# A fused cosine attention and two-layer MLP on one core: one pair's normalisation moved behind another quad's scalings, two transposes moved to later groups, weight loads asked for ahead of squares

## The chip, the cores and the metric

The kernel runs on one core of a Trainium2 chip. The metric is the device time of one execution in microseconds (us), lower is better; where several executions were timed, their median is given. The core's engines are TensorE (PE in the profile: matmuls, and PEld for its weight loads), VectorE (DVE), ScalarE (ACT), GpSimd (POOL) and SyncE (SP), which only issues transfers (DMAs). Each engine works through its own list of instructions in order; semaphores make it wait for others.

## The reference

```python
batch, n_heads, seq, head_dim = (8, 12, 448, 64)          # q, k, v
n_tokens, d_model, d_ff = (3584, 768, 2048)               # w_in, w_out
...
q_n = q / (np.linalg.norm(q, axis=-1, keepdims=True) + 1e-06)
k_n = k / (np.linalg.norm(k, axis=-1, keepdims=True) + 1e-06)
scores = np.matmul(q_n, k_n.transpose(0, 1, 3, 2)) / tau
attn = softmax of scores over the keys
attn_out = np.matmul(attn, v)
...
x = attn_out as (batch * seq, heads * head_dim)
h = x @ w_in
g = np.maximum(0.01 * h, h)
out = g @ w_out
```

All inputs are float32, tau is 0.1. Scores of normalised vectors are bounded, so the kernel takes the exponential without subtracting the maximum.

## The kernel before

**Units of work.** Two heads of one batch are a *pair* (48 pairs, `NSLOT`; six per batch), two pairs are a *quad* of four heads (`j`, three per batch). The 448 positions of a head are three blocks of 128 and a rest of 64. Pairs are counted from 0 through the whole kernel: pairs 0 to 5 are batch 0, pair 6 (the seventh) is the first of batch 1. Quad 2 is the last of batch 0.

**Preparing a pair `s`.** Its queries and keys are loaded in float32 into `raw_sb` (six places, used in turn). GpSimd squares them (`squares`, L173 to L184, two operations, one for queries, one for keys and each with part of the rest); VectorE sums each row (`sums`, L186, two reductions); ScalarE takes the root as exp(0.5 ln x) (`roots`, L197). `normalise` (L213 to L228) then runs on VectorE: an addition (L217), a reciprocal (L218) and two multiplications that write the normalised bf16 tile `qn` (L222, 128x512 and 128x384; called the pair's *scalings* here). `transposes` (L248) turns `qn` over: for pairs below 10 by seven small TensorE products (L236) into one bank of PSUM and a copy by VectorE (L260) into `qkT`; from pair 10 on (`DMA_FROM`) by a DMA that SyncE issues. `norm` (L700 to L717) strings these together and lets GpSimd go on: `hold` (L511) is a tiny GpSimd copy that reads a value of `qn[s]`, so all that stands behind it in GpSimd's list waits for that pair's scalings; behind it come squares of a later pair and, for pairs 7 and 8, a quarter of `w_out`.

**Attention.** `key_tiles` (L267) makes the scores of key blocks, keys on the partitions (L279), and ScalarE takes their exponential (L291). The rest blocks of two pairs share a tile (`ki` of 3), which so needs `qkT` of both: the tile called (7, 3) reads pairs 6 and 7, the tile (9, 3) reads pairs 8 and 9. `attend` (L660) sums the exponentials by products with ones and multiplies them with `v` (L319); ScalarE forms the reciprocals `rb` (L338, L339) and VectorE scales the result into `xT` (`scale`, L355 to L362, instruction at L360): the attention output with features on the partitions. Quad 2 fills the last two of the six feature blocks.

**The MLP.** `first` (L374) multiplies one block `m` of 128 of the 2048 inner features: six products (L383), one for each feature block, then ScalarE's leaky ReLU into `hT` (L390). `firsts` (L719) goes through all 16 blocks, called *groups* below; a table `between` says what is emitted ahead of which group. The first four groups of batch 0 (`SOON`) have their first four products done earlier, and need only the last two, those that read quad 2's part of `xT`. `groups` (L441) does the second layer (L458) and `visit` (L729) mixes it with the key tiles of the next batch: first the tiles (7, 3) and (9, 3), then groups of output rows with a key tile every few products.

**Order.** Nothing is left to a scheduler (`manual_schedule`): the order on every engine is the order of emission. PSUM has eight banks, and `banks` (L75) gives out those whose last use was longest ago. GpSimd also issues DMAs: `w_in`, the queries and keys of pairs 10 and 11 (L584 to L586), `w_out` in four quarters named by their first block 0, 4, 8 and 12 (`load_w_out`, L109; the reader is L458), and `v`. SyncE issues the other loads and the stores.

**Around the change.** At the end of batch 0 the list is: `sums(6)`, `sums(7)`, `roots(6)`, `normalise(6)` (L655 to L658); `attend` of quad 2 (L751), with its scalings at the end; a `hold` on `xT`, `w_out` quarter 0, a `hold` on `qn[6]`, `squares(9)`, quarter 4 (L752 to L756); `norm(7)` without its transposes, with `squares(10)` and quarter 8; `sums(8)`; and then the 16 groups of batch 0 with the table at L760 to L769, in which `transposes(6)` to `transposes(9)`, `norm(8)` to `norm(10)` and their sums are spread. Squares 10 and 11 can only begin when their pairs have been loaded.

Of the kernel before, what the change touches and what calls it, by code (L numbers as in the profile page):

```python
# [16 lines left out]
def kernel(  # L17
# [57 lines left out]
    def banks(count, keep=None, which=None):  # L75
        lo, hi = (0, 8) if not deals["apart"] else (0, 4) if count == 2 else (4, 8)
        x = which if which is not None else min(
            (i for i in range(lo, hi, count) if not set(range(i, i + count)) & set(sum(kept.values(), []))),
            key=lambda i: max(age[i : i + count]),
        )  # L80
        deals["n"] += 1
        age[x : x + count] = [deals["n"]] * count
        if keep:
            kept[keep] = list(range(x, x + count))
        return ps[:, x] if count == 1 else ps[:, x : x + count]

    def given_back(keep):
        deals["n"] += 1
        for i in kept.pop(keep):
            age[i] = deals["n"]  # L90
# [18 lines left out]
    def load_w_out(parts):  # L109
        for m in parts:  # L110
            gp.dma_start(out=w_out_sb[:, m : m + MT // 4], in_=w_out_r[:, m : m + MT // 4])

    def main(x, b, h0, nh):
        return x[b, h0 : h0 + nh, 0:MAIN].rearrange("h (p t) d -> p h t d", t=3)
# [40 lines left out]
    def load_v(j):  # L155
        if j >= B * NQ:
            return
        b, jj = divmod(j, NQ)
        vb[j] = vbp.tile([128, 4, 3, D], BF16, name="v_b")
        gp.dma_start(out=vb[j], in_=main(v, b, 4 * jj, 4))  # L160
# [25 lines left out]
    def sums(s, parts=(0, 1)):  # L186
        if s >= NSLOT:
            return
        if s not in ss:
            ss[s] = smp.tile([128, 14], F32, name="ss")  # L190
        for i in parts:
            o = ss[s][:, 0:8] if i == 0 else ss[s][:, 8:14]
            nc.vector.tensor_reduce(  # L193
                o.rearrange("p (h t) -> p h t", h=2), sqs[s][i], axis=AX.X, op=ALU.add
            )

    def roots(s):  # L197
        if s >= NSLOT:
            return
        nc.scalar.activation(ss[s], ss[s], func=AF.Ln, bias=tiny)  # L200
        nc.scalar.activation(ss[s], ss[s], func=AF.Exp, scale=0.5)  # L201
# [11 lines left out]
    def normalise(s):  # L213
        if s >= NSLOT:
            return
        r = smp.tile([128, 14], F32, name="r")
        nc.vector.tensor_scalar_add(ss[s], ss[s], 1e-6)  # L217
        nc.vector.reciprocal(r, ss[s])  # L218
        qn[s] = qnp.tile([128, 7, 2, D], BF16, name="qn")
        for x, lo, hi, r0 in ((raw[s][0], 0, 4, 0), (raw[s][1], 4, 7, 8)):  # L220
            nt = hi - lo
            scalings[s] = nc.vector.tensor_tensor(  # L222
                qn[s][:, lo:hi],
                x.rearrange("p h t d -> p t h d"),
                r[:, r0 : r0 + 2 * nt].rearrange("p (h t) -> p t h", h=2)
                .unsqueeze(3).to_broadcast([128, nt, 2, D]),
                op=ALU.mult,
            )  # L228
# [5 lines left out]
    def one(tp, s, lo, hi):  # L234
        for t in range(lo, hi):
            nc.tensor.matmul(  # L236
                out=tp[:, t, :],
                lhsT=qn[s][:, t].rearrange("p h d -> p (h d)"),
                rhs=id128,
                is_transpose=True,  # L240
                start=(t == lo),
                stop=(t == hi - 1),
            )

    def transposed():
        return banks(1).bitcast(BF16)[:, : 7 * 128].rearrange("p (t c) -> p t c", c=128)

    def transposes(s):  # L248
        if s >= NSLOT:
            return  # L250
        dst = qtp.tile([128, 7, 128], BF16, name="qkT")
        qkT[s] = dst.rearrange("p t c -> p (t c)")
        if s >= DMA_FROM:
            nc.sync.dma_start(
                out=dst, in_=qn[s].rearrange("p t h d -> p (t h d)"), transpose=True
            )
            return
        tp = transposed()
        one(tp, s, 0, 7)
        nc.vector.tensor_copy(out=dst, in_=tp)  # L260
# [67 lines left out]
    def totals(j, sm=None):  # L328
        rem = None if sm is not None else lambda g: ones_rem[:, rem_half(j, g)]
        sms[j] = banks(1) if sm is None else sm  # L330
        strip_products(j, sms[j], lambda g, ki: ones, rem)
        if sm is not None:
            reciprocals(j)

    def reciprocals(j):
        sm = sms.pop(j)
        rb = rbp.tile([128, S], F32, name="rb")
        nc.scalar.activation(rb, sm[:, :S], func=AF.Ln)  # L338
        nc.scalar.activation(rb, rb, func=AF.Exp, scale=-1.0)  # L339
        rbs[j] = rb  # L340
# [3 lines left out]
    def products(j, e, po=None, begun=False):  # L344
        b, jj = divmod(j, NQ)
        if po is None:
            po = banks(1, (j, e))
        pos[j, e] = po
        vm = vb[j].rearrange("p h t (d e) -> p h t e d", e=2)
        vr = vrb[b % 2].rearrange("p j g (d e) -> p j g e d", e=2)  # L350
        strip_products(
            j, po, lambda g, ki: vm[:, g, ki, e], None if begun else lambda g: vr[:, jj, g, e]
        )

    def scale(j, e):  # L355
        b, jj = divmod(j, NQ)
        m, half = divmod(b, 2)
        if m not in xT:
            xT[m] = xtp.tile([128, KT, 2 * S], BF16, name="xT")
        scalings[j, e] = nc.vector.tensor_tensor(  # L360
            xT[m][:, 2 * jj + e, half * S : (half + 1) * S], pos.pop((j, e))[:, :S], rbs[j],
            op=ALU.mult,  # L362
        )
        if (j, e) in kept:
            given_back((j, e))
# [3 lines left out]
    def chunk_cols(c):  # L369
        return (0, MAIN) if c % 2 == 0 else (MAIN, 512)  # L370
# [3 lines left out]
    def first(c, m, kts=range(KT)):  # L374

        c0, n = chunk_cols(c)
        if c not in hT:
            hT[c] = htp.tile([128, MT, 512], BF16, name="hT")
        if (c, m) not in pms:
            pms[c, m] = banks(1)  # L380
        pm = pms[c, m]
        for kt in kts:
            nc.tensor.matmul(  # L383
                out=pm[:, :n],
                lhsT=w_in_sb[:, kt, m * 128 : (m + 1) * 128],
                rhs=xT[c // 2][:, kt, c0 : c0 + n],
                start=(kt == 0), stop=(kt == KT - 1),
            )
        if kts[-1] == KT - 1:
            nc.scalar.activation(  # L390
                out=hT[c][:, m, :n], in_=pms.pop((c, m))[:, :n], func=AF.Prelu, alpha=0.01
            )
            if (c, m, 0) in kept:
                given_back((c, m, 0))
# [116 lines left out]
    def hold(x):  # L511
        seen = smp.tile([128, 1], F32, name="seen")
        gp.tensor_copy(out=seen, in_=x)  # L513
# [141 lines left out]
    sums(6)  # L655
    sums(7)
    roots(6)
    normalise(6)  # L658

    def attend(j, behind=()):  # L660
        totals(j)
        reciprocals(j)
        po = banks(2)
        for e in range(2):
            products(j, e, po[:, e])
        for fn in behind:
            fn()
        for e in range(2):
            scale(j, e)
# [30 lines left out]
    def norm(s, transposed=True):  # L700
        if s >= NSLOT:
            return
        roots(s)
        normalise(s)
        if transposed:
            transposes(s)
        if s == 10:
            return
        for x in (12, 13) if s == 11 else (s + 4,) if s > 11 else ():
            load_qk(x)  # L710
        hold(qn[s][:, 6, 0, 0:1])
        if s == 11:
            squares(12)
        if s != 9:
            squares(s + (3 if s < 9 else 2))
        if s < 9:
            load_w_out((4 * (s - 5),))  # L717

    def firsts(b, begun, between):  # L719

# [8 lines left out]
    def visit(b, order, norms, between):  # L729
# [5 lines left out]
        for i, pairs in enumerate(order):  # L735
# [13 lines left out]

    deals["apart"] = False  # L750
    attend(NQ - 1, [lambda m=m: first(0, m, range(KT - 2)) for m in range(3, SOON)])  # L751
    hold(xT[0][:, 2 * NQ - 2, 0:1])  # L752
    load_w_out((0,))
    hold(qn[6][:, 6, 0, 0:1])
    squares(9)
    load_w_out((4,))  # L756
    norm(7, False)
    sums(8)
    firsts(
        0, SOON, {  # L760
            3: [lambda: transposes(6)],
            4: [lambda: norm(8, False)],
            5: [lambda: sums(9), lambda: transposes(7)],
            8: [lambda: norm(9, False)],
            9: [lambda: transposes(8)],
            10: [lambda: sums(10), lambda: load_v(3)],
            12: [lambda: norm(10), lambda: load_v(4)],
            13: [lambda: transposes(9), lambda: load_v(5), lambda: load_v_rem(1)],
            15: [lambda: sums(11)],  # L769
# [3 lines left out]
    for b in range(B):  # L773
# [21 lines left out]
        s = ready  # L795
# [57 lines left out]
```

## Time and profile before

| | |
|---|---|
| Median of 3 executions | 409.48 us (409.43 to 411.63) |
| The profiled execution's own time | 409.33 us |
| Its span, from first to last instruction | 407.5 us |
| Granted TensorE clock | 1.00 |
| ScalarE, VectorE, GpSimd busy | 65%, 47%, 35% of the span |
| TensorE products L383, first layer | 768, 148.2 us |
| TensorE products L458, second layer | 1536, 143.0 us |
| VectorE scalings L222 | 96, 58.8 us, mean 654 ns |
| GpSimd squares L182 | 92, 84.3 us, mean 937 ns |

A row of the timeline gives the start, the time taken, the engine, the line of the kernel, the operation, what is written and read, how many instructions were merged in the row, and in brackets the idle time ahead of it with what ended that. The chain of waits goes back from the last instruction and names at each step what released it: start, length, what. An engine may be busy while its instruction does not get on, for instance when it waits for a port; the duration is then longer than that of the same form elsewhere.

### The profile page before, as it was taken

To read this page: it belongs to the slowest core of one execution; us is meant where nothing else is said; L and a number is where in the kernel's file an instruction comes from. 1 tells how busy PE (TensorE), PEld (TensorE's weight loads), DVE (VectorE), ACT (ScalarE), POOL (GpSimd) and SP (SyncE) were. 2 spreads that over 40 slices of the span, in tenths; PEclk is the share of its full clock that TensorE was granted. 3 is DMA by queue.
4 is the path that set the end of the run, shared out by engine and by line. 5 is a ranking of instruction groups with operands and counts; after the bars stand their busy time and mean duration, and the time that the engine had idled before them with its cause. 6 is when DMAs were issued, how large, how long until landed. Compare 5 with 4: busy or idle time off the path is not lost.

```text
span 407.5 us, 10171 instructions
## 1 busy us (share of the span) xinstructions
PE 399.7 (98%) x4096; PEld 213.5 (52%) x4096; DVE 190.3 (47%) x405; ACT 263.1 (65%) x454; POOL 142.8 (35%) x218
## 2 busy tenths in 40 slices
PE   8899999999999999999999999999999999999996
PEld 3334655544555655544555555544555555554564
DVE  6889931771644624354542635257261645130021
ACT  5995689565865688745876569845876559944300
POOL 5897643371323422253241614055231530000000
PEclk9999999999999999999999999999999999999999
DMA  7999999594695958187386958485468733210033
GB/s 185 240 228 240 211 184 228 157 205 109 136 205 78 151 80 218 49 132 173 76 164 156 124 126 161 114 117 139 92 172 163 110 75 63 63 41 2 0 78 78
DMA packets 100735, 54.21 MB, mean 133 GB/s; under 512 B 69424, under 2 KB 95440, under 8 KB 100688
## 3 DMA queue, kind: packets, MB, share of 16 engines
q1 hardware_dynamic: 76400, 40.13, 43.0%
q0 software_dynamic: 23440, 12.92, 23.4%
q8 instruction: 32, 0.52, 0.5%
q10 hardware_dynamic: 848, 0.52, 0.4%
q14 instruction: 15, 0.12, 0.1%
HBM read 45.61 MB, written 11.01 MB: 139 GB/s over the span
## 4 chain that ended last, share of the span: by engine, by line
PE 92%; DVE 3%; POOL 2%; DMA 1%; issue 1%; ACT 0%; POOLq 0%
PE ps L383 35%; PE ps L458 31%; PE ps L319 11%; PE ps L279 8%; PE ps L420 5%; DVE qn L222 2%; PE ps L306 1%; POOL sq L182 1%; DMA raw_sb<-in_k_dram 1%; PE ps L236 0%; POOL raw_sb L132 0%; POOL v_rem L167 0%; DVE qkT L260 0%; DVE xT L360 0%; DVE r L218 0%
## 5 line engine op out<-in xcount | busy, mean ns | idle before, releaser
L383 PE MATMUL ps<-xT,w_in_sb 128*128 128x384 bf16 (+1 forms) x768 | 148.2, 353 | 0.4 <-DVE xT L360 0.4
L458 PE MATMUL ps<-w_out_sb,hT 64*128 64x384 bf16 x1536 | 143.0, 323 | 0.0
L291 ACT ACTIVATE pe<-ps 128x896 bf16<-128x896 f32 x144 | 123.9, 918 | 19.9 <-PE ps L279 17.6
L390 ACT ACTIVATE hT<-ps 128x384 bf16<-128x384 f32 (+1 forms) x128 | 67.4, 542 | 69.9 <-PE ps L383 69.6
L383 PEld LDWEIGHTS <-w_in_sb 128*128 128x128 bf16 x768 | 74.1, 98 | 72.2 <-issue 4.6
L458 PEld LDWEIGHTS <-hT 64*128 64x128 bf16 x1536 | 73.5, 94 | 55.1 <-PE ps L458 4.1
L182 POOL TENSOR_TENSOR sq<-raw_sb 128x512 f32<-128x512 f32 x92 | 84.3, 937 | 15.9 <-DMA raw_sb<-in_k_dram 15.1
L222 DVE TENSOR_TENSOR qn<-raw_sb,r 128x512 bf16<-128x512 f32 x96 | 58.8, 654 | 1.9 <-DMA raw_sb<-in_q_dram 0.3
L470 DVE COPY osb<-ps 128x384 f32<-128x384 f32 x41 | 21.2, 553 | 74.5 <-PE ps L458 44.0
L279 PE MATMUL ps<-qkT 64*128 64x448 bf16 (+1 forms) x384 | 54.6, 354 | 1.1 <-DVE qkT L260 0.6
L193 DVE TENSOR_REDUCE ss<-sq 128x6 f32<-128x384 f32 (+1 forms) x95 | 54.3, 610 | 2.0 <-POOL sq L182 1.9
L513 POOL CAST seen<-qn 128x1 f32<-128x1 bf16 x47 | 9.3, 197 | 124.1 <-DVE qn L222 123.9
L217 DVE TENSOR_SCALAR ss<-ss 128x14 f32<-128x14 f32 x48 | 9.9, 207 | 70.9 <-ACT ss L201 70.7
L360 DVE TENSOR_TENSOR xT<-ps,rb 128x448 bf16<-128x448 f32 x48 | 27.7, 619 | 24.2 <-ACT rb L339 24.0
L160 POOL DMA_DIRECT2D v_b<-in_v_dram x24 | 18.5, 774 | 54.8 <-PE ps L319 54.8
L319 PE MATMUL ps<-pe,v_b 128*32 128x448 bf16 x576 | 32.0, 353 | 0.0
L279 PEld LDWEIGHTS <-qkT 64*128 64x128 bf16 (+1 forms) x384 | 16.3, 96 | 20.7 <-issue 8.1
L426 DVE COPY osb<-ps 128x384 f32<-128x384 f32 (+1 forms) x9 | 4.6, 513 | 36.6 <-issue 22.6
L291 ACT ACTIVATE pr<-ps 128x896 bf16<-128x896 f32 x24 | 21.3, 922 | 0.2 <-PE ps L279 0.2
L319 PEld LDWEIGHTS <-v_b 128*32 128x32 bf16 x576 | 15.1, 97 | 11.9 <-issue 0.6
L338 ACT ACTIVATE rb<-ps 128x448 f32<-128x448 f32 x24 | 12.9, 537 | 12.7 <-PE ps L319 11.8
L420 PE MATMUL ps<-w_out_sb,hT 128*128 128x384 bf16 (+1 forms) x144 | 21.0, 308 | 0.0
(50 smaller groups left out, 188.1 us busy)
## 6 DMA issues: line engine op xcount, KB each, us to landing
raw_sb<-in_q_dram SPq DMA_DIRECT2D x46, 192.0 KB, 3.4
raw_sb<-in_k_dram SPq DMA_DIRECT2D x44, 192.0 KB, 3.5
out_dram<-osb SPq DMA_DIRECT2D x30, 192.0 KB, 2.8
v_b<-in_v_dram POOLq DMA_DIRECT2D x24, 192.0 KB, 4.7
out_dram<-osb SPq DMA_DIRECT2D x12, 384.0 KB, 2.8
w_out_sb<-in_moe_w_out_dram POOLq DMA_DIRECT2D x4, 768.0 KB, 11.2
w_in_sb<-in_moe_w_in_dram POOLq DMA_DIRECT2D x3, 512.0 KB, 8.7
w_in_sb<-in_moe_w_in_dram POOLq DMA_DIRECT2D x2, 768.0 KB, 13.9
```

The costliest lines, as they stand in the source:

```text
L182: eng.tensor_tensor(sq, x, x, op=ALU.mult)
L193: nc.vector.tensor_reduce(o.rearrange("p (h t) -> p h t", h=2), sqs[s][i], axis=AX.X, op=ALU.add)
L222: scalings[s] = nc.vector.tensor_tensor(qn[s][:, lo:hi], x.rearrange("p h t d -> p t h d"), r[:, r0 : r0 + 2 * nt].rearrange("p (h t) -> p ...
L279: nc.tensor.matmul(out=out[:, a, :S], lhsT=x[rows, c0:c1], rhs=x[rows, 0:S], start=True, stop=True,)
L291: nc.scalar.activation(out=dst, in_=sc[:, :, :S], func=AF.Exp, scale=inv_tau)
L319: nc.tensor.matmul(out=x[32 * g : 32 * g + 32, :S], lhsT=weights(g, ki) if ki < 3 else rem(g), rhs=pe[s][:, ki, a, :] if ki < 3 else pr[j] ...
L360: scalings[j, e] = nc.vector.tensor_tensor(xT[m][:, 2 * jj + e, half * S : (half + 1) * S], pos.pop((j, e))[:, :S], rbs[j], op=ALU.mult,)
L383: nc.tensor.matmul(out=pm[:, :n], lhsT=w_in_sb[:, kt, m * 128 : (m + 1) * 128], rhs=xT[c // 2][:, kt, c0 : c0 + n], start=(kt == 0), stop= ...
L390: nc.scalar.activation(out=hT[c][:, m, :n], in_=pms.pop((c, m))[:, :n], func=AF.Prelu, alpha=0.01)
L420: nc.tensor.matmul(out=po2[:, :n], lhsT=hT[c][:, m, ts * 128 : (ts + 1) * 128], rhs=w_out_sb[:, m, lo : lo + n], start=(m == 0), stop=(m = ...
L458: done[p][i] = nc.tensor.matmul(out=pos2[p][:, i, :HALF], lhsT=hT[c][rows, m, ts * 128 : (ts + 1) * 128], rhs=w_out_sb[rows, m, half * HAL ...
L470: copy(out=osb[c, ts][:, half * HALF : (half + 1) * HALF], in_=po2[:, i, :HALF])
```

## The change

- `normalise(6)` is emitted behind `attend` of quad 2, that is behind quad 2's two scalings on VectorE, instead of ahead of `attend`.
- `w_out`'s quarters 0 and 4 are asked for together, ahead of the `hold` on `qn[6]` and of `squares(9)`. In `norm`, the quarter (8 for pair 7, 12 for pair 8) is asked for ahead of the squares (10 and 11) instead of behind them.
- In the table, `transposes(6)` goes from ahead of group 3 to group 4, `transposes(7)` from 5 to 7, `transposes(8)` from 9 to 10; `sums(9)` from 5 to 6, `norm(9)` from 8 to 9, `sums(10)` and `load_v(3)` from 10 to 11. `norm(8)`, `norm(10)`, `transposes(9)` and `sums(11)` stay.

```diff
     roots(6)
-    normalise(6)
...
         hold(qn[s][:, 6, 0, 0:1])
+        if s < 9:
+            load_w_out((4 * (s - 5),))
         if s == 11:
             squares(12)
         if s != 9:
             squares(s + (3 if s < 9 else 2))
-        if s < 9:
-            load_w_out((4 * (s - 5),))
...
     attend(NQ - 1, [lambda m=m: first(0, m, range(KT - 2)) for m in range(3, SOON)])
+    normalise(6)
     hold(xT[0][:, 2 * NQ - 2, 0:1])
-    load_w_out((0,))
+    load_w_out((0, 4))
     hold(qn[6][:, 6, 0, 0:1])
     squares(9)
-    load_w_out((4,))
     norm(7, False)
     sums(8)
     firsts(
         0, SOON, {
-            3: [lambda: transposes(6)],
-            4: [lambda: norm(8, False)],
-            5: [lambda: sums(9), lambda: transposes(7)],
-            8: [lambda: norm(9, False)],
-            9: [lambda: transposes(8)],
-            10: [lambda: sums(10), lambda: load_v(3)],
+            4: [lambda: transposes(6), lambda: norm(8, False)],
+            6: [lambda: sums(9)],
+            7: [lambda: transposes(7)],
+            9: [lambda: norm(9, False)],
+            10: [lambda: transposes(8)],
+            11: [lambda: sums(10), lambda: load_v(3)],
             12: [lambda: norm(10), lambda: load_v(4)],
```

## The prediction

> **What bounds the kernel now.** I read the page first, then the chain of waits from 30 to 56 us, then the timeline of 28 to 60 us. All times are us from the start of the span.
>
> ```profile
> span 407.5 us, 10171 instructions
> PE 399.7 (98%) x4096; PEld 213.5 (52%) x4096; DVE 190.3 (47%) x405; ACT 263.1 (65%) x454; POOL 142.8 (35%) x218
> ```
>
> TensorE (PE) is busy for 399.7 of 407.5 us, and the page gives its granted clock as full in every slice. The change moves no work off TensorE, so all that it can win is idle time of TensorE in the stretch it touches. The chain of waits through that stretch:
>
> ```profile
> 34.67 0.54 DVE qn L222
> 35.21 1.07 DVE xT L360 x2
> ...
> 36.66 2.95 DVE qn L222 x2
> ...
> 39.66 0.34 PE ps L236 x3
> 40.00 3.90 PE ps L383 x24
> ...
> 48.58 2.92 PE ps L383 x18
> 51.51 0.64 PE ps L279 x8
> ```
>
> From 34.7 to 39.6 the chain lies on VectorE (DVE): scalings of pair 6 (L222), xT (L360), scalings of pair 7. Then it lies on TensorE until the first key tiles at 51.5. So TensorE waits at two places, both before 39.7. Now the timeline:
>
> ```profile
> 33.94 0.58 ACT L339 ACTIVATE rb<-rb 128x448 f32<-128x448 f32 x1
> 35.80 0.32 PE L383 MATMUL ps<-xT,w_in_sb 128*128 128x384 bf16 x1 [0.21 <-DVE xT L360]
> 36.33 0.97 PE L383 MATMUL ps<-xT,w_in_sb 128*128 128x384 bf16 x5 [0.21 <-DVE xT L360]
> 36.66 2.94 DVE L222 TENSOR_TENSOR qn<-raw_sb,r 128x512 bf16<-128x512 f32 x2
> 37.37 1.82 POOL L182 TENSOR_TENSOR sq<-raw_sb 128x512 f32<-128x512 f32 x2
> 39.66 0.34 PE L236 MATMUL ps<-id,qn 128*128 128x128 bf16 x3 [0.45 <-DVE qn L222]
> 44.62 2.29 POOL L182 TENSOR_TENSOR sq<-raw_sb 128x512 f32<-128x512 f32 x2 [4.47 <-DMA raw_sb<-in_k_dram]
> 45.09 2.23 DVE L222 TENSOR_TENSOR qn<-raw_sb,r 128x512 bf16<-128x512 f32 x2
> 51.09 0.62 DVE L260 COPY qkT<-ps 128x896 bf16<-128x896 bf16 x1
> 51.76 0.11 PEld L279 LDWEIGHTS <-qkT 64*64 64x64 bf16 x4 [0.21 <-DVE qkT L260]
> ```
>
> Read the brackets: 0.21 + 0.21 for xT, 0.45 for the last tiles of pair 7. That is 0.87 us, 0.21% of the time. The last two rows matter most: VectorE's copy of the ninth pair's transposes ends at 51.71, and the second key tile starts at 51.76, after a weight load that waited 0.21 for that copy. At 51.7 VectorE is thus no earlier than TensorE: what TensorE wins ahead of that point waits there, unless VectorE's list comes earlier too.
>
> **Part 1: normalise(6) behind the xT scalings.** The reciprocal rb is there at 33.94 + 0.58 = 34.52. The xT scalings now start at 35.13, behind pair 6's (34.05 + 1.16 = 35.21, the two overlapping a little). Afterwards they start at 34.57 and end at 35.72, 0.55 earlier. TensorE's first waiting product, at 35.80 now, follows straight on at 35.42 (it repeats every 0.1625: 3.90 us for 24). The next needs the second half at 35.72 and starts at 35.77 in place of 36.33: TensorE is 0.55 ahead.
>
> The price falls on VectorE, which idles from 32.36 to 34.57 instead of working on pair 6 from 33.16. Pair 6 now follows xT: 0.16 + 0.24 + 1.16 with the gaps between 36.19 and 36.66 makes its end 37.27. TensorE has seven products left, reaches transposes(6) (now in group 4) at 35.77 + 7 x 0.1625 = 36.91, does four tiles and waits 0.2 for the second scaling. They end at 37.50.
>
> **Part 2: pair 7 against the squares.** GpSimd's (POOL's) squares(9) are held back by pair 6's end: 37.27 + a hold of 0.18 gives 37.51 (now 37.37). Pair 7's addition and reciprocal take VectorE to 37.67. The two then collide throughout. How that is paid is in the rows: at 36.66 one scaling was done before, and the other ended 0.42 after both squares (37.37 + 1.82 = 39.19); at 45.09 scalings and squares took turns and the scalings ended 2.70 after the squares' start. By turns pair 7 ends at 37.51 + 2.70 = 40.21; behind both squares, which end at 37.51 + 1.82 = 39.33, at 39.33 + 1.03 = 40.4 (1.03 is what the scalings at 86.64, shown below, took after the squares ahead of them had ended at 87.06). I take the turns, as at 45.09 the squares were likewise first by a few tenths. Now it is 39.60, so VectorE is 0.6 to 0.9 later; without a collision it would end at 38.83, 0.8 earlier than now.
>
> **Part 3: the turnings later.** transposes(7) go from group 5 to 7: TensorE gets there at 37.50 + 18 x 0.1625 = 40.42, pair 7 is about there, and the wait of 0.45 is gone. transposes(8) go to group 10: 40.42 + 0.39 + 2.93 = 43.74 (now 43.74 by chance, but a group further on). So TensorE is 0.97 ahead, one group of six products. VectorE's list from pair 7's end to pair 9's scalings (sums, copy, pair 8, sums, copy) is unchanged in kind; now it runs from 39.60 to 45.09 with 0.2 of gaps, so pair 9's addition comes at 44.60 + 0.6 = 45.2 or later. ScalarE (ACT) hides its part: the roots of pair 8 hold back three activations to about 41.8, and group 4's is over at 41.8 + 0.5 = 42.3; its bank comes round only at 43.7, after seven others. Had it to be used again by group 8 at 41.8, TensorE would wait 0.5.
>
> Squares(10) stay at 44.62, since they wait for the load of pairs 10 and 11. Now pair 9's addition is done just ahead of them; afterwards it falls into them. The trace has the same case 40 us later:
>
> ```profile
> 85.17 1.89 POOL L182 TENSOR_TENSOR sq<-raw_sb 128x512 f32<-128x512 f32 x2
> 85.80 0.53 DVE L217 TENSOR_SCALAR ss<-ss 128x14 f32<-128x14 f32 x1 [0.62 <-ACT ss L201]
> 86.64 1.45 DVE L222 TENSOR_TENSOR qn<-raw_sb,r 128x512 bf16<-128x512 f32 x2
> ```
>
> The addition came 0.63 after the squares' start, took 0.53 (0.17 uncontended), and the scalings ended at 88.09, 2.92 after the squares' start. So pair 9 ends at 44.62 + 2.92 = 47.54, now 45.09 + 2.23 = 47.32: 0.22 later. Bounds: had the scalings the same turn as now, 0.0; if the addition must let both squares go first (46.45), 46.45 + 0.33 + 1.16 = 47.94, 0.62. I take 0.22, from the nearest row.
>
> **Where the gain goes.** After pair 9 VectorE's list is a chain: copy 8, sums(10), roots, pair 10, copy 9 (47.32 to 51.71 now). Copy 9 ends at 51.93 and the second key tile starts at 51.98, 0.22 later than now. TensorE meanwhile waits about 0.3 in transposes(9) (47.06 to 47.6), finishes the groups at about 50.7, does the first key tile and stands idle for about 0.9 us. The 0.55 and 0.45 that it won are given back there.
>
> **Part 4: w_out.** (Quarters are named by their first block: 0, 4, 8, 12.) Quarter 4 is issued at about 36.3 instead of 39.14, quarter 8 at about 40.4 instead of 46.85; each costs GpSimd 0.81. They move past squares(9), (10) and (11). Squares(9) wait for pair 6 anyhow (37.27, both issues done by 37.1); squares(10) wait for their load; squares(11) start within 0.4 of now. Gain: the four issues land 8.6 to 12.5 us after issue, behind the load of pairs 10 and 11 on the same queue, so asking earlier lands nothing sooner. I take zero; at most quarter 12 lands 2.6 us earlier (asked for at about 47.0, not 49.58), which only the products of the second layer from 52 us on could use, and in the view of that tile they wait 0.2 in all. The loss is rival (b). SyncE's list is the same, and the banks that the later key tiles take were given back longer ago, not shorter.
>
> Quarter 4's issue (36.3 to 37.1) now lies beside pair 6's scalings (36.11 to 37.27). Nearest row: an issue at 49.58 took its usual 0.81 beside the scalings of pair 10 from 50.01, so the price is nothing and squares(9) start at 37.51. The Trainium skill, SBUF — State Buffer, section "SBUF: two separate sides", warns that GpSimd cannot write the descriptors of its own DMAs while VectorE runs an operation in a 2-port mode. Taken to hold for these scalings, it would give 408.8 in place of 409.7, by rival (a); the row at 49.58 does not show it.
>
> **Sum.** 409.33 (the profiled execution; span 407.5 and 1.8 around it) + 0.22 = 409.55; the median is 0.15 above that execution, so 409.7. With the bounds 0.0 and 0.62: 409.4 to 410.2 with a little for noise.
>
> **Rivals.** (a) The gain stays. If scalings and squares collide less, pair 7 ends up to 0.8 earlier than now, pair 9 goes ahead of squares(10), and TensorE keeps what it won, at most 0.87 + the 0.13 at 51.7: 408.5 to 409.2, say 408.8. For it: VectorE idles 0.62 before pair 10. One way to it: were quarter 4's issue held up until pair 6 ends at 37.27, it would be over at 38.1, squares(9) start at 38.3, and pair 7's first scaling, from 37.67, pass ahead of them. Against: the undisturbed issue at 49.58, and that every collision in the trace cost. 0.25, of which 0.05 by that way.
>
> (b) Slower: the early w_out quarters take bandwidth from the load of pairs 10 and 11. Between 36.0 and 44.6 the DMA view shows 254 GB/s and the engines full; one quarter of 768 KB is 3.1 us at that rate. If one is served ahead of the load, squares(10) end at 49.6, sums(10) at 50.7 instead of 48.91, and all after is 1.8 later: 411.3; with two quarters 414.4. It counts from a start of squares(10) after about 45.9 (sums(10) start at 47.78 now, and the squares take 1.82). Against it: now, too, quarter 0 is asked for 8 us before that load is in, and w_out lands only after it. 0.05.
>
> (c) The change does nothing in the end: VectorE in step with now, copy 9 at 51.7, the time within 0.1 of 409.5. That is the lower edge of my forecast and is counted in it.
>
> **Numbers.** Forecast 0.70, (a) 0.25, (b) 0.05. A measurement of this kernel can tell about 1%, 4.1 us, from no change. Only (b) with two quarters reaches that: slower 0.02; faster would need 4 us of idle time that the stretch does not have: 0.01; within 0.97. The range leaves out the far ends of (a) and (b): 408.8 to 410.6.
>
> **What would show it.** Right: no wait for xT above 0.2 at 35.8; xT scalings from 34.6; pair 7's scalings over 2 us, ending after 40; TensorE waiting 0.5 to 1.1 us for L260 just before 52. Wrong: copy 9 before 51.3 (rival a), or squares(10) starting after 45 (rival b).

## The result and the profile after

| | executions | median us | range | ratio to before, 95% interval |
|---|---|---|---|---|
| before | 22 | 409.44 | 408.44 to 411.63 | |
| changed | 22 | 411.45 | 409.11 to 413.17 | 1.0033 (1.0017 to 1.0048) |

The change made the kernel slower: the medians lie 2.0 us apart, and the ratio over all runs, which takes in how the times spread, is 1.0033. 409.7 was forecast, with 410.6 as the upper end. The times of the changed kernel form two groups: four executions between 409.11 and 409.19, eighteen between 410.96 and 413.17, none between. Both groups are undisturbed executions of the same program. The kernel before has them too, but with the numbers the other way round: four of its 22 lie above 411. The profile of the changed kernel is of an execution of 412.14 us, in its upper group; that of before (409.33 us) lies with the majority of its own executions.

The page of the profile after, the lines that answer to those of before:

```profile
span 410.4 us, 10159 instructions
PE 401.1 (98%) x4086; PEld 213.9 (52%) x4096; DVE 191.0 (47%) x405; ACT 262.7 (64%) x454; POOL 143.2 (35%) x218
PEclk9999989999999999999999999999999999999999
```

The span is 2.9 us longer. TensorE does the same work in it, and one of the 40 slices has not quite the full clock. The chain of waits from 30 to 56 us (start, length, what):

```profile
34.58 1.16 DVE xT L360 x2
...
36.13 1.16 DVE qn L222 x2
...
37.68 2.63 DVE qn L222 x2
...
45.31 0.55 DVE ss L217
...
46.16 3.31 DVE qn L222 x2
49.46 0.05 issue
49.51 0.34 PE ps L236 x3
49.85 4.60 PE ps L383 x18
54.45 0.50 PE ps L279 x8
```

Before, the chain left VectorE at 39.6. Now it stays on VectorE until 49.5, but for ScalarE's roots of pairs 8 and 9: xT, pairs 6, 7, 8 and 9, one after another. The row at 46.16 is pair 9's two scalings, 3.31 us where the same form takes 1.16 alone. The timeline there shows what they ran into:

```profile
43.99 1.82 POOL L182 TENSOR_TENSOR sq<-raw_sb 128x512 f32<-128x512 f32 x2 [2.27 <-DMA raw_sb<-in_k_dram]
45.31 0.54 DVE L217 TENSOR_SCALAR ss<-ss 128x14 f32<-128x14 f32 x1
45.76 0.17 POOL L513 CAST seen<-qn 128x1 f32<-128x1 bf16 x1
45.89 0.81 POOL L111 DMA_DIRECT2D w_out_sb<-in_moe_w_out_dram  x1
46.16 3.30 DVE L222 TENSOR_TENSOR qn<-raw_sb,r 128x512 bf16<-128x512 f32 x2
46.72 2.31 POOL L182 TENSOR_TENSOR sq<-raw_sb 128x512 f32<-128x512 f32 x2
48.41 0.40 PE L236 MATMUL ps<-id,qn 128*128 128x128 bf16 x4 [1.17 <-DVE qn L222]
49.51 0.34 PE L236 MATMUL ps<-id,qn 128*128 128x128 bf16 x3 [0.70 <-DVE qn L222]
```

Squares(10) began at 43.99, 0.63 earlier than in the profile of before, since their load had landed earlier. Pair 9's addition (45.31) was held up by them until 45.85. When its scalings were asked for at 46.16, squares(10) were over; but squares(11), the next in GpSimd's list behind quarter 12's issue (45.89), went first. The first square ended at 47.77, and VectorE's first scaling at 48.36, 2.20 us after it had been asked for; its second took its turn after the second square (over at 49.03). TensorE stood idle for 1.17 and 0.70 us at transposes(9). After that its granted clock went to half, as the view by stretches has it (the number behind the five engines' columns is the clock; from 50 to 51 it reads 0.57, from 53 to 54 0.73):

```profile
49.00:50.00 1.00, 0.49 (x5) 0.38 (x6) 1.00 (x3) 0.00 (x0) 0.22 (x2) 1.00 1.18 214
...
51.00:52.00 1.00, 1.00 (x5) 0.44 (x3) 0.34 (x3) 0.90 (x4) 1.00 (x2) 0.50 1.19 217
...
54.00:55.00 1.00, 1.00 (x13) 0.32 (x13) 0.89 (x2) 0.51 (x2) 0.18 (x1) 1.00 1.14 206
```

So the 18 products that took 2.92 us before took 4.60.

### The profile page after: what moved, and what is told of

It reads as the page before. It is cut to its first block, busy times and chain, and to the rows that moved or that the text cites. A ratio compares the mean times of both kernels' runs of the same rounds, so it can differ in the third digit from the quotient of the medians.

```text
span 410.4 us, 10159 instructions
## 1 busy us (share of the span) xinstructions
PE 401.1 (98%) x4086; PEld 213.9 (52%) x4096; DVE 191.0 (47%) x405; ACT 262.7 (64%) x454; POOL 143.2 (35%) x218
## 4 chain that ended last, share of the span: by engine, by line
PE 89%; DVE 5%; POOL 2%; issue 1%; DMA 1%; ACT 1%; POOLq 0%
PE ps L383 33%; PE ps L458 31%; PE ps L319 11%; PE ps L279 8%; PE ps L420 5%; DVE qn L222 3%; PE ps L306 1%; POOL sq L182 1%; DMA raw_sb<-in_k_dram 1%; DVE ss L193 1%; DVE r L218 0%; POOL raw_sb L132 0%; DVE ss L217 0%; POOL v_rem L167 0%; DVE xT L360 0%
## 5 line engine op out<-in xcount | busy, mean ns | idle before, releaser
L200 ACT ACTIVATE ss<-ss,tiny 128x14 f32<-128x14 f32 x48 | 14.8, 307 | 11.7 <-DVE ss L193 11.3
L338 ACT ACTIVATE rb<-ps 128x448 f32<-128x448 f32 x24 | 12.9, 538 | 12.7 <-PE ps L319 11.8
```

## The experiments

Theory A: pair 9's scalings came late enough to meet squares(11) as well as squares(10), and each of the squares can hold the port for a turn. Theory B: it is the issue of w_out's quarter between the two squares that holds them. Theory C: the later turnings bring TensorE into a long wait and cost it its clock.

### One part at a time

x1, the changed kernel with w_out's order undone:

```diff
-    load_w_out((0, 4))
+    load_w_out((0,))
     hold(qn[6][:, 6, 0, 0:1])
     squares(9)
+    load_w_out((4,))
...
         if s != 9:
             squares(s + (3 if s < 9 else 2))
+        if s < 9:
+            load_w_out((4 * (s - 5),))
```

> The changed kernel with w_out's quarters asked for behind the squares again (0, squares(9), 4, squares(10), 8, squares(11), 12). Theory A, squares(11) take the port: in the profile of the changed kernel pair 9's scalings are asked for at 46.16, after squares(10) are over, and then wait for squares(11). Here squares(11) still come within about 1 us of squares(10), so the loss stays: 410.5 to 412, pair 9's scalings end after 48.5. Theory B, the issue of quarter 12 between squares(10) and (11) is what holds the scalings: 409.2 to 409.8, scalings over by 47.6.

Measured: 411.14 median of 12, ratio 1.0028 (1.0010 to 1.0046); seven executions above 411, five at 409.2 to 409.9. w_out's order is not needed for the loss. Its profile fell on an execution of 409.37, so the expected end of the scalings after 48.5 could not be seen in it. Nor does x1 tell theory A from theory B: with the old order it is the issue of quarter 8 that stands between squares(10) and (11). That is left to x2.

x3, the kernel before with normalise(6) alone moved:

```diff
     roots(6)
-    normalise(6)
...
     attend(NQ - 1, [lambda m=m: first(0, m, range(KT - 2)) for m in range(3, SOON)])
+    normalise(6)
```

> The kernel before with normalise(6) moved behind attend, and nothing else: the old table and the old places of w_out. Theory A: VectorE is as late as in the changed kernel, pair 9 meets squares(10) and (11) again: 410.3 to 412. Theory C, the later turnings are the cause (TensorE comes earlier to a wait and loses its clock): 409.2 to 409.7, no slice below full clock.

Measured: 411.16 median of 12, ratio 1.0033 (1.0018 to 1.0047), seven of twelve above 411. The old table does not save it, so theory C falls as the cause of the whole.

x4, the kernel before with w_out's order alone changed:

```diff
-    load_w_out((0,))
+    load_w_out((0, 4))
     hold(qn[6][:, 6, 0, 0:1])
     squares(9)
-    load_w_out((4,))
...
         hold(qn[s][:, 6, 0, 0:1])
+        if s < 9:
+            load_w_out((4 * (s - 5),))
```

> The kernel before with only w_out's quarters asked for ahead of the squares. Theory A: pair 9's scalings are asked for at about 45.1 as before and take their turn inside squares(10): 409.2 to 409.8, as before. Theory B: the issue between squares(10) and (11) costs here too: 410.3 or above.

Measured: 411.19 median of 12, ratio 1.0029 (1.0011 to 1.0046), eight of twelve above 410.9. Theory A expected 409.2 to 409.8 and missed. Its profile (411.25) and that of one more execution, l4 (408.71), show why:

> The kernel before with only w_out's order changed, for a second profile. Theory A: slow (410.9 to 412) if squares(10) start before about 44.2, fast (409.4 to 409.8) with scalings inside squares(10) if they start after about 44.4.

In x4's profile, around pair 7:

```profile
36.27 1.56 POOL L111 DMA_DIRECT2D w_out_sb<-in_moe_w_out_dram  x2
36.89 3.33 DVE L222 TENSOR_TENSOR qn<-raw_sb,r 128x512 bf16<-128x512 f32 x2
37.96 1.84 POOL L182 TENSOR_TENSOR sq<-raw_sb 128x512 f32<-128x512 f32 x2
```

In l4's, the same instructions:

```profile
35.91 1.56 POOL L111 DMA_DIRECT2D w_out_sb<-in_moe_w_out_dram  x2
36.53 1.16 DVE L222 TENSOR_TENSOR qn<-raw_sb,r 128x512 bf16<-128x512 f32 x2
37.77 1.82 POOL L182 TENSOR_TENSOR sq<-raw_sb 128x512 f32<-128x512 f32 x2
```

Two issues now lie ahead of squares(9). The issues and the scalings of l4 lie 0.36 us before those of x4, so the lists ran in the same order; what differs is pair 9's load, which squares(9) need. In l4 it was asked for at 24.73 and landed 12.9 us later, at 37.6: until then the squares could not start, the scalings passed, and the pair took 1.16. In x4 it was asked for at 23.82 and landed 10.0 us later, at 33.8: squares(9) stood ready behind the issues, and the second scaling, asked for at 37.50, waited for both of them (3.33 for the pair). There pair 9 came to 45.91 and met squares(11) as well, as in the changed kernel. So at pair 7, too, the landing of a load decides. In l4 pair 9 was done at 44.82, before squares(10) even started (44.96); so the time was low as expected, and below what was expected, since there was no turn to wait for at all.

### Taking squares(11) away

x2, the changed kernel with squares(11) behind pair 9's scalings:

```diff
-        if s != 9:
+        if s != 8:
             squares(s + (3 if s < 9 else 2))
```

> The changed kernel with squares(11) emitted behind pair 9's scalings and their hold. Theory A: no squares are left beside pair 9's scalings once squares(10) are over; they end by 47.6, copy 9 near 51.8, every run at 409.0 to 409.8 and the granted clock full. Theory B: the issue of quarter 12 still lies beside them, and 0.5 us or more is lost: 409.9 or above, scalings over 1.6 us.

Measured: 409.35 median of 11, ratio 0.9998 (0.9986 to 1.0010), all between 408.99 and 410.15. The upper group is gone. Its profile, with the load as early (squares(10) at 43.97) and the issue at the same place:

```profile
45.15 0.67 DVE L217 TENSOR_SCALAR ss<-ss 128x14 f32<-128x14 f32 x1
45.87 0.81 POOL L111 DMA_DIRECT2D w_out_sb<-in_moe_w_out_dram  x1
46.13 1.16 DVE L222 TENSOR_TENSOR qn<-raw_sb,r 128x512 bf16<-128x512 f32 x2
47.58 1.82 POOL L182 TENSOR_TENSOR sq<-raw_sb 128x512 f32<-128x512 f32 x2
51.73 0.38 PE L279 MATMUL ps<-qkT 64*64 64x448 bf16 x4 [0.80 <-DVE qkT L260]
```

The scalings ran in 1.16 beside the issue, so theory B falls: the issue alone does not hold them. The last row is the second key tile: TensorE waits 0.80 there for VectorE's copy 9, as forecast.

### The same program twice

> The changed kernel once more, for one profile. Theory A with the load's landing as the trigger: if squares(10) start before about 44.2, pair 9's scalings are asked for after them, wait for squares(11) and end after 48.5, time 410.9 to 412.5; if squares(10) start after about 44.4, the scalings take a turn inside them, end by 47.8, time 409.0 to 409.8. A profile with an early start and an early end of the scalings, or the reverse, speaks against it.

> The changed kernel a third time, the same two cases: squares(10) before about 44.2 with scalings over after 48.5 and 410.9 or more, or after about 44.4 with scalings over by 47.8 and 409.8 or less.

l1 took 409.19 us, l2 411.62. From l1:

```profile
44.33 1.82 POOL L182 TENSOR_TENSOR sq<-raw_sb 128x512 f32<-128x512 f32 x2 [2.77 <-DMA raw_sb<-in_k_dram]
45.16 0.24 DVE L217 TENSOR_SCALAR ss<-ss 128x14 f32<-128x14 f32 x1
45.71 1.47 DVE L222 TENSOR_TENSOR qn<-raw_sb,r 128x512 bf16<-128x512 f32 x2
51.62 0.38 PE L279 MATMUL ps<-qkT 64*64 64x448 bf16 x4 [0.81 <-DVE qkT L260]
```

From l2:

```profile
44.15 1.82 POOL L182 TENSOR_TENSOR sq<-raw_sb 128x512 f32<-128x512 f32 x2 [2.55 <-DMA raw_sb<-in_k_dram]
45.20 0.81 DVE L217 TENSOR_SCALAR ss<-ss 128x14 f32<-128x14 f32 x1
46.32 3.29 DVE L222 TENSOR_TENSOR qn<-raw_sb,r 128x512 bf16<-128x512 f32 x2
46.88 2.31 POOL L182 TENSOR_TENSOR sq<-raw_sb 128x512 f32<-128x512 f32 x2
48.57 0.40 PE L236 MATMUL ps<-id,qn 128*128 128x128 bf16 x4 [1.44 <-DVE qn L222]
```

Squares(10) started 0.18 us apart (44.33 lies between the two bounds that were expected, 44.2 and 44.4). In l1 the addition was asked for at 45.16, while the first of them ran (to 45.36), and got its turn between the two. In l2 the first ended at 45.18; the addition, at 45.20, was too late, waited for the second (to 45.97), and the scalings then found squares(11) ahead of them. The same program loses 2.4 us or not, by 0.2 us in the landing of one load. x1 once more:

> The changed kernel with w_out behind the squares again, for a second profile. Theory A: in a slow execution squares(10) start before about 44.2, the first scaling passes beside the issue of quarter 8 and the second waits for both squares(11), ending after 48.5, 410.9 to 412; in a fast one squares(10) start later and all is over by 47.6, 409.2 to 409.9.

It took 409.44 us, with squares(10) at 44.40: the lower group again. What the upper group of x1 and of x3 waits for was thus not seen in a profile.

### The clock

x5, the changed kernel with four dummy products ahead of transposes(9):

```diff
-            13: [lambda: transposes(9), lambda: load_v(5), lambda: load_v_rem(1)],
+            13: [lambda: fill(4), lambda: transposes(9), lambda: load_v(5), lambda: load_v_rem(1)],
```

> The changed kernel with four dummy products of 512 columns on TensorE (results unused) ahead of transposes(9), where it idled 1.17 and 0.70 us and where the clock went to half for 3.4 us afterwards. Theory A with the clock as a second part: the collision of pair 9 with squares(11) stays, so most runs stay at 410.9 to 411.8, but the runs above 412 go and no run's granted clock is below 0.998. Rival: the clock fell for another reason than the idle time, then about a third of the runs stay above 411.9 with a clock of 0.994 to 0.996.

Measured: 411.08 median of 12, ratio 1.0028 (1.0012 to 1.0044), seven above 411, none above 411.78, no clock below 0.998. In the changed kernel six of 22 executions lay at 412.01 to 413.17, all with a clock of 0.994 to 0.996, and no other execution had one below 0.998. That agrees, but with twelve executions it is a hint rather than proof. l2 idled 1.44 and 0.70 us at the same place and kept its full clock.

### Where the gain went, and a faster version

x6, all squares behind the scalings (squares(9) behind pair 7's, 10 and 11 behind pair 9's):

```diff
-    hold(qn[6][:, 6, 0, 0:1])
-    squares(9)
...
+        if s == 7:
+            squares(9)
         if s < 9:
             load_w_out((4 * (s - 5),))
+        if s == 9:
+            squares(10)
         if s == 11:
             squares(12)
-        if s != 9:
-            squares(s + (3 if s < 9 else 2))
+        if s > 8:
+            squares(s + 2)
```

> The changed kernel with squares(9) emitted behind pair 7's scalings and squares(10) and (11) behind pair 9's. Theory A (every collision of scalings and squares costs VectorE up to two squares): pair 7 ends at 38.9, pair 9 near 45.5, copy 9 near 51.2; 408.7 to 409.2, all runs together, some 0.3 us faster than before. Rival (the load of pairs 10 and 11 or the sums are what VectorE's list waits for): 409.2 to 409.8, no gain over the kernel with squares(11) alone moved.

Measured: 409.28 median of 12, ratio 0.9992 (0.9979 to 1.0006). The rival was right: pair 9 ended at 45.67, as expected, but the sums then waited for squares(10), which could only start at 45.95, and copy 9 ended at 51.59, only 0.09 before that of x2 (51.68).

x8, x2 with copy 9 alone by ScalarE (in `transposes`):

```diff
-        nc.vector.tensor_copy(out=dst, in_=tp)
+        if s == 9:
+            nc.scalar.copy(out=dst, in_=tp)
+        else:
+            nc.vector.tensor_copy(out=dst, in_=tp)
```

> The changed kernel with squares(11) behind pair 9's scalings, and only copy 9 done by ScalarE. In that kernel TensorE waited 0.80 us for VectorE's copy 9 behind pair 10's scalings. Theory (the gain of the change is given back exactly there): 408.4 to 408.8, the wait gone. Rival: the next wait takes it at once, at the same tile or at w_out: 409.1 or above.

Measured: 408.56 median of 12, ratio 0.9975 (0.9964 to 0.9986). The wait of 0.80 is gone, and the median is 0.79 us under that of x2. Its profile also repeats what x2 showed: the addition was asked for at 45.25, 1.02 after the start of squares(10), took 0.82 beside them in place of 0.17, and the scalings behind it still took 1.16.

x7, x6 with copies 6 to 9 by ScalarE (`if s > 5`):

> The kernel with all squares behind the scalings, and the copies of transposes 6 to 9 done by ScalarE in place of VectorE. Theory A with VectorE's list as the bound: the copies leave VectorE, copy 9 no longer stands behind pair 10's scalings, TensorE no longer waits at the second key tile, and the gain of the change shows: 408.2 to 408.7. Rival (TensorE would meet w_out's last quarter or ScalarE's list at once): 409.0 or above.

Measured: 408.27 median of 12, all within 408.10 to 408.65, ratio 0.9971 (0.9958 to 0.9984): faster than both kernels, 1.1 us under its runs of before (409.34). Its two key tiles and the copy that the second needs:

```profile
49.79 0.90 ACT L261 COPY qkT<-ps 128x896 bf16<-128x896 bf16 x1
50.84 0.57 PE L282 MATMUL ps<-qkT 64*64 64x448 bf16 x8
```

Eight products in one row: TensorE no longer waits between the tiles.

## Why the prediction was wrong

**Right, step by step.** xT from 34.57 (measured 34.58); pair 6 done at 37.27 (37.29); pair 7 by turns at 40.21 (40.31); TensorE at transposes(7) at 40.42 (40.45) and at transposes(8) at 43.74 (43.76); pair 9's addition at 45.2 (45.16 to 45.31); TensorE giving its gain back at the second key tile, idle for about 0.9 (0.80 in x2, 0.81 in l1). x8 shows the last causally: with that one copy off VectorE's list, 0.79 us come back. Against rival (a), the collision at pair 7 was there in the changed kernel's profile and in l1 and l2. Against rival (b), squares(10) started between 43.75 and 44.96 in the eleven other profiles in which only the load held them, in the median at 44.2 with w_out asked for early and (with the kernel before) at 44.5 without; 45.9 was never reached.

**The step that failed.** "Squares(10) stay at 44.62": they do not stay: the load lands anywhere in those 1.2 us, and I took one execution's landing for a constant. With it went the choice of the nearest row. The row at 85.80, with the addition 0.63 after the squares' start, is the case of l1 (0.83 after it, still inside the first square). There pair 9 ended 2.85 after the squares' start (2.92 in the row), and, as they started at 44.33, at 47.18: 0.14 earlier than before, not 0.22 later. The time was 409.19. In the changed kernel's profile and in l2 the addition came 1.32 and 1.05 after the start, behind the first square.

**The bound that failed with it.** For that case I had put an end, pair 9 at 47.94, 0.62 late. Measured: 46.16 + 3.30 = 49.46 and 46.32 + 3.29 = 49.61, 2.1 to 2.3 us later than before, whence the 2.0 us. The bound let both squares(10) go first and then gave VectorE the port. But squares(11) were in GpSimd's list behind them, and in the row at 85.80 no further squares were. "Squares(11) start within 0.4 of now" stood under part 4 as a cost of nothing. They started at 46.72 in the changed kernel's profile and at 46.88 in l2, against 47.81 before: 1.09 and 0.93 earlier, since squares(10) started earlier and, with no scaling between them, took 1.82 in place of 2.29. That was the place of the loss, as x2 shows by moving them: with the load as early and the addition as late, pair 9 took 1.16.

The Trainium skill, SBUF — State Buffer, section "SBUF: two separate sides", says of the port pair that whichever of the two starts first gets it for the whole instruction. The rows of l1 and l2 agree: 0.2 us decide who is first, and the loser waits a whole square. The recorded starts alone do not follow it: at 46.16 the scaling is recorded 0.56 us ahead of squares(11) and still went second (see the last section). What decided here is the whole list behind the squares, and the spread of what starts it.

**Clock.** The halved clock was in no term. It cost TensorE 4.60 - 2.92 = 1.68 us; of this about 0.68 reached the end. Copy 9 was done at 53.84, but TensorE came to the key tiles only at 54.38 and to the second layer at 54.89, 1.05 after the copy; in l1 and l2, at full clock, it was there 0.37 after it (51.56 to 51.93, 54.00 to 54.37).

The Trainium skill, TensorE: Matmul & The Clock Gate, Part 1, has the clock go to half after an idle window of about 3.4 us. Here the longest single wait was 1.17 us and the two together 1.87; the half clock lasted about 3.4 us. Read as 3.4 us without a product, that rule would not have halved the clock here; the measurement decides, and l2 shows that such waits do not always bring it.

**What stays open.** Why four of 22 executions of the kernel before (and four and seven of 35 in later sets) lie in an upper group: the same collision would do it (by the same 2 us), but no profile of one was taken. And why the parts differ (four of 22 before; seven or eight of twelve with one or two of the parts undone; eighteen of 22 with all) may come from two places of collision, each with a load whose landing decides: at pair 9 the load of pairs 10 and 11, at pair 7 that of pair 9. In the profiles of x1 and x5, both of the lower group, squares(9) waited 0.21 and 1.16 us for pair 9's load, pair 7 was done at 39.59 and 38.56 (40.31 in the changed kernel's profile), and pair 9's addition came before squares(10). The chances were not counted out; x5, with all parts, had seven of twelve, so some of the difference to eighteen of 22 may be chance.

## What to carry to other kernels

A gain on the bounding engine is worth what the next meeting point with another engine leaves of it: look for that point first, and ask whether the other engine's list comes earlier too. Where two engines exclude each other at a port, a price read from one execution holds only as long as the order of arrival does; take the spread of whatever starts the one of them, and count everything that stands ready behind it. A median can hide two groups of executions, so the list of times is worth reading before the profile of one.

## What the runs showed of the hardware

- GpSimd's squares seem to hold the port before their own row begins, when they stand ready behind a DMA issue: in the changed kernel a scaling asked for at 46.16 waited 0.56 us before squares(11) were recorded at 46.72, while in x2, with a waiting instruction behind the same issue, it ran at once. The same 0.56 to 0.57 stands at pair 9 in l2 and x4. What takes the port was not isolated.
- Even VectorE's small addition (128x14) waits: 0.17 us alone, 0.81 in l2. Reductions beside squares kept their 1.13 to 1.14 (x2, at 47.74).
- GpSimd's DMA issue took 0.81 us beside scalings (x2) as it did without them.
- ScalarE's copy of a turned pair (128x896) took 0.90 to 0.92 us against VectorE's 0.61, and was still the better place for it.
